# A Hyena-style mixer plus token MLP on one core: 16-bit sine phases, the state kernel loaded first, tap diagonals on GpSimd, and a new written-out order

## The chip, the cores and the metric

The kernel runs on one core of a Trainium2 chip. The core has a matrix engine (PE in the profile, with its weight loads as PEld), a vector engine (DVE), a scalar engine (ACT), a general engine (POOL, also called GpSimd) and SP, which here only issues DMAs. Each engine works through its own queue strictly in order, and the engines meet only through semaphores. The metric is the device time of one execution in microseconds; the kernel before has a median of 170.74 us over three runs (170.0 to 171.14).

## The reference

Two blocks, S = 2048 positions, D = 448 channels, F = 1792. All arrays are bf16.

```python
# block A, x = A_q:  q = layernorm(x)
k_shift = sum over t of k[s - t] * shift_k[:, 3 - t]      # 4 taps per channel
kv = k_shift * v
y  = causal convolution of kv with ssm_k, length 2048 (written as FFTs of length 4096)
y  = bf16(y) + kv * ssm_D
h  = x + q * y
# block B: z = layernorm(layernorm(h))
u  = gelu_tanh(einsum("bsd,sf->bdf", z, w1) + b1)         # mixes positions, not channels
out = h + transpose(einsum("bdf,fs->bds", u, w2) + b2)
```

## The kernel before

Position s is split as s = 16 q + r: q (0 to 127) is the partition, r (0 to 15) a row of 448 channels. All on-chip storage is one big array (`arena`), all matrix results lie in eight banks of `ps`, used singly or in pairs.

The long convolution is a two-stage Fourier transform done with matrix multiplies. Its pieces, named by the tags that the code and the text use:

- **tables** builds the sine and cosine tables: `E` (stage one, 32 tables of 128x128, made by the Sin function on ACT from integer phases that DVE prepares), `FW`, `MA`, `MB`, `MN` (stage two and its inverse), and the identity `ID`. The small tables need `pcf`, a column of bit fields of the partition number, which DVE makes in five short steps (L822 to L831); POOL then forms their phases (L854, L858), ACT takes the sine (L862), and POOL multiplies by a mask (L871).
- **loads** and **xload** fetch `ssm_k` (the state kernel, `KN`, four pieces), `k`, `v` and `x` (four pieces of 448 KB each), the taps and the biases. SP issues them.
- **kT** transposes the state kernel on PE (L1037), evicted by DVE or ACT.
- **kv** transposes `k` on PE (L965) into `KX`, and applies the four taps as PE multiplies with 64x64 diagonal matrices `DG` (L991); DVE multiplies the result by `v` (L1006). `DG` is an identity times the taps (L950, one DVE instruction of 128x1024).
- **k1**, **u1**: stage one of the transform, of the state kernel and of `kv`, 16 groups each (L1058), evicted to a ring of four buffers, mostly by ACT (L1068; four groups of k1 by DVE, L1066, which adds D there). For every second group three DMAs (L1074; two issued by POOL, one by SP) shuffle the ring into `TK` or `TU`.
- **k2**, **u2**: stage two (L1093), 16 steps each; the two results of a pair of steps go to ACT and DVE for eviction (L739, L742, L741).
- **i1**: DVE multiplies the two transforms (L1160, 16 products of 1.02 us apart), PE does the first inverse stage (L1177), ACT and DVE evict, and DMAs (L1201, and L1188 for the last pair) shuffle into `TZ`.
- **i2**: the second inverse stage for each r (L1303, L1309), followed by the gate with q and the two layer norms (DVE, ACT and POOL), which give `Q[r]`. The statistics of x (**q**, `bn_stats`, L1237) and four normalised rows (**xn**) are independent of the convolution.
- **mlp**: the two matrix products, 112 + 112 matmuls for the first (L1435, L1445), gelu on ACT (L1425), 238 for the second (L1457), the final add on DVE (L1460).

A step such as `k1.5` is the group 5 of its tag, and `k1.5:8` is instruction 8 of the step (here the eviction). The order of every engine's queue is written out by hand in the table `ORDER`, and the banks that each step takes in `SLOTS`; the replay in `schedule` (L297) follows both and only derives the waits from them. So a change of `ORDER` is a change of the program order on every engine.

## Time and profile before

| | us |
|---|---|
| median of three runs | 170.74 |
| profiled execution, span from first to last instruction | 168.7 |
| difference between the two | 2.0 |
| first k1 eviction on ACT starts | 14.32 |
| first k2 matmul starts | 34.96 |
| first i1 product on DVE starts | 50.05 |
| last i1 eviction on ACT ends | 70.83 |
| first mlp matmul starts | 78.25 |
| last mlp matmul's result reaches DVE | 165.81 |

The span is what the profiler saw of one execution, and its own time is that span; the runs are timed from outside and lie 2.0 us above it. Times in the text are counted from the span's start. A duration in a row is that of the instruction alone; instructions of one engine overlap a little, so that a row "x3 2.52" means 0.84 us for each in a sequence, where a single one shows 0.92. The granted clock of TensorE is 1.00 in all parts of the span.

### The profile page before, as it was taken

To read this page: it belongs to the slowest core of one execution; us is meant where nothing else is said; L and a number is where in the kernel's file an instruction comes from. 1 tells how busy PE (TensorE), PEld (TensorE's weight loads), DVE (VectorE), ACT (ScalarE), POOL (GpSimd) and SP (SyncE) were. 2 spreads that over 40 slices of the span, in tenths; PEclk is the share of its full clock that TensorE was granted. 3 is DMA by queue.
4 is the path that set the end of the run, shared out by engine and by line. 5 is a ranking of instruction groups with operands and counts; after the bars stand their busy time and mean duration, and the time that the engine had idled before them with its cause. 6 is when DMAs were issued, how large, how long until landed. Compare 5 with 4: busy or idle time off the path is not lost.

```text
span 168.7 us, 3563 instructions
## 1 busy us (share of the span) xinstructions
...
## 2 busy tenths in 40 slices
...
GB/s 142 421 310 385 286 278 348 312 355 132 211 134 325 248 197 186 196 152 290 388 402 400 424 421 422 418 112 0 0 0 12 46 54 54 54 2 56 54 54 54
DMA packets 15564, 35.15 MB, mean 208 GB/s; under 512 B 3804, under 2 KB 9644, under 8 KB 15548
## 3 DMA queue, kind: packets, MB, share of 16 engines
...
q10 hardware_dynamic: 144, 0.08, 0.2%
q14 instruction: 5, 0.04, 0.1%
...
## 4 chain that ended last, share of the span: by engine, by line
PE 62%; ACT 15%; DVE 10%; DMA 6%; issue 3%; POOL 1%; DVEq 0%; ACTq 0%; POOLq 0%
PE ps L1457 25%; PE ps L1435 13%; PE ps L1445 13%; ACT arena L738 7%; DMA arena<-arena 6%; ACT arena L1068 4%; ACT arena L739 4%; DVE arena L1160 2%; PE ps L1309 2%; PE ps L1058 2%; PE ps L1037 2%; PE ps L1093 2%; DVE arena L741 2%; DVE arena L837 1%; PE ps L1177 1%
## 5 line engine op out<-in xcount | busy, mean ns | idle before, releaser
L1460 DVE SCALAR_TENSOR_TENSOR arena<-ps,arena 128x448 bf16<-128x448 f32 (+2 forms) x17 | 11.1, 656 | 55.8 <-PE ps L1457 55.8
L1457 PE MATMUL ps<-arena 128*128 128x448 bf16 (+2 forms) x238 | 42.7, 342 | 0.0
L1457 PEld LDWEIGHTS ps<-arena 128*128 128x128 bf16 x238 | 33.3, 145 | 9.5
L1435 PE MATMUL ps<-arena 128*128 128x448 bf16 x112 | 23.5, 353 | 0.0
L738 ACT CAST arena<-ps 128x896 bf16<-128x896 f32 (+1 forms) x29 | 23.1, 933 | 0.0
L1068 ACT CAST arena<-ps 128x896 bf16<-128x896 f32 x24 | 20.2, 920 | 4.8 <-PE ps L1058 3.3
L1445 PE MATMUL ps<-arena 128*128 128x448 bf16 x112 | 22.3, 352 | 0.0
L1074 POOL DMA_DIRECT2D arena<-arena x32 | 17.7, 558 | 8.6 <-ACT arena L1068 8.5
L1425 ACT ACTIVATE arena<-ps,arena 128x448 bf16<-128x448 f32 x14 | 8.2, 632 | 19.3 <-PE ps L1445 10.3
L1093 PE MATMUL ps<-arena 128*64 128x448 bf16 x128 | 15.3, 361 | 2.0 <-ACT arena L739 0.9
L1435 PEld LDWEIGHTS ps<-arena 128*128 128x128 bf16 x112 | 10.7, 98 | 10.8 <-DVE arena L1388 1.3
L1445 PEld LDWEIGHTS ps<-arena 128*128 128x128 bf16 x112 | 11.0, 98 | 10.2
L1160 DVE TENSOR_TENSOR arena<-arena 128x1792 bf16<-128x1792 bf16 x16 | 16.5, 1084 | 0.0
L1177 PE MATMUL ps<-arena 64*128 64x448 bf16 x128 | 14.1, 351 | 1.1 <-ACT arena L738 0.5
L1058 PE MATMUL ps<-arena 128*32 128x448 bf16 x256 | 14.6, 355 | 0.5 <-ACT arena L1068 0.2
L1201 POOL DMA_DIRECT2D arena<-arena x16 | 9.3, 586 | 13.8 <-ACT arena L738 12.9
L1093 PEld LDWEIGHTS ps<-arena 128*64 128x64 f16 x128 | 5.3, 108 | 11.2 <-ACT arena L739 3.4
L1177 PEld LDWEIGHTS ps<-arena 64*128 64x128 f16 x128 | 5.2, 94 | 9.8 <-DVE arena L1160 3.1
L1388 DVE TENSOR_SCALAR arena<-arena 128x448 bf16<-128x448 f32 x16 | 7.6, 509 | 4.8 <-POOL arena L1381 4.8
L1058 PEld LDWEIGHTS ps<-arena 128*32 128x32 f16 x256 | 5.1, 95 | 7.8 <-ACT arena L1068 2.6
L1237 DVE BATCH_NORM_STATS2 arena<-arena 128x6 f32<-128x448 bf16 x16 | 9.4, 612 | 0.0
L739 ACT ACTIVATE arena<-ps 128x896 bf16<-128x896 f32 x10 | 8.6, 926 | 0.8 <-PE ps L1093 0.8
...
## 6 DMA issues: line engine op xcount, KB each, us to landing
...
```

Of the source, the lines that this page charges most:

```text
L738: return e.copy(out=dst(), in_=src())
L739: return e.activation(out=dst(), in_=src(), func=ACT.Copy, scale=scale)
L1058: op("pe", lambda e, W, b=b, r=r, q=q, x=x, c0=c0: e.matmul(PS[32 * q:32 * q + 32, b.slots[x], 0:D], E[:, 2 * r + x, c0:c0 + 32], src[:, r ...
L1068: return e.copy(out=dst, in_=Ppair(b)) if W == "act" else e.tensor_copy(out=dst, in_=Ppair(b))
L1074: shuf[tag].append(op(q_, lambda e, W, g=g, i=i, a=a, nu=nu, jh=jh: e.dma_start(T[a + i:a + i + 4 * nu - 3:4].rearrange("p (j k) c d -> p ...
L1093: op("pe", lambda e, W, b=bs[h], h=h, j=j, c=c, par=par: e.matmul(PS[64 * par:64 * par + 64, b.slots[c], 0:D], FW[:, 64 * c:64 * c + 64], ...
L1160: op("dve", lambda e, W, m=m, i=i: e.tensor_tensor(out=MR(m.slots[0]).rearrange("p (x y) d -> p x y d", x=2), in0=TU[:, i].unsqueeze(2).br ...
L1177: k = op("pe", lambda e, W, b=bs[h], m=ms[h], par=par, t=t, tab=tab, xy=xy, P=P: e.matmul(Pb(b, par), tab[P, :], MR(m.slots[0])[P, xy, :], ...
L1435: op("pe", lambda e, W, r=r, fc=fc, b=bs[fc]: e.matmul(Pb(b), W1A[:, r, 128 * fc:128 * fc + 128], Q[:, r, :], start=(r == 0), stop=(r == R ...
L1445: op("pe", lambda e, W, r=r, fc=fc, b=b: e.matmul(Pb(b), W1B[:, r, 128 * (fc - n0):128 * (fc - n0) + 128], Q[:, r, :], start=(r == 0), sto ...
L1457: op("pe", lambda e, W, r=r, fc=fc, b=b, d0=d0, d1=d1: e.matmul(Pb(b)[:, d0:d1], W2[fc // 7][:, fc % 7, r:S:R], G[:, fc, d0:d1], start=(fc ...
L1460: op("dve", lambda e, W, r=r, b=b, A=A, d0=d0, d1=d1: e.scalar_tensor_tensor(out=XR(r)[:, d0:d1], in0=Pb(b)[:, d0:d1], scalar=bm[:, r:r + ...
```

## The change

Four edits and a new order.

1. **Phases of `E` in 16 bits.** Before, DVE computes the phase of every table as a 32-bit product of 1024 elements, adds a quarter period, and masks, each twice. Now it computes one row of 128 as a 16-bit product, doubles the number of rows four times by 16-bit additions (128, 256, 512 and 1024 elements), and masks and shifts in six 16-bit instructions of 1024 elements. ACT takes the sines in four instructions of 1024 elements in place of two of 2048.
2. **Taps.** They are loaded as four contiguous rows by DMAs that ACT issues, transposed on PE (four small matmuls, `kv.0`) and evicted to `wsc`; POOL's cast goes. The diagonals `DG` may be made by DVE or POOL, and `ORDER` gives them to POOL.
3. **Loads.** The pieces of the state kernel are loaded ahead of three of the four pieces of `k`, one piece of x ahead of all of `v` and a second ahead of three of its four pieces; the biases later.
4. **b2** is used as bf16 (a DVE cast of 16 elements goes).
5. **`ORDER` and `SLOTS` are new on all engines.** k1 comes ahead of nearly all of the tap matmuls and u1; the table `FW`, its relatives and `pcf` come later; bn_stats of the first two pieces of x come earlier, others later; the small shuffles of i1 go behind the last large ones; the matmuls of the MLP are interleaved over r and over blocks.

```diff
 ORDER = {
     "pe": (
-        "dummy.0:1-9 kv.4:0-11 kv.3:0-7 kv.6:0-11 kv.5:0-7 kT.1:0-7 kT.0:0-3 kT.1:9-11 kT.0:4-7 kT.3:0-7 "
+        "dummy.0:1-9 kv.2:0-7 kv.3:0-11 kv.0:0 kT.0:0-7 kT.1:0-7 kT.1:9 kT.4:0-7 kT.1:10-11 kT.5:0-7 kT.2:0-7 "
...
-            for h in range(2):
-                sch.t0 = T_TH if h else -40.0
-                o_ph = (o_pi, o_TK)[h]
-                ph = view(o_ph, [2, 8, 128], i32)
-                op("dve", lambda e, W, h=h, ph=ph: e.tensor_tensor(
-                    out=ph[:, 1], in0=frow.unsqueeze(1).broadcast_to([128, 8, 128]),
-                    in1=srow[:, 8 * h:8 * h + 8].unsqueeze(2).broadcast_to([128, 8, 128]), op=ALU.mult),
-                   r=[(o_fr, 512), (o_s, 64)], w=[(o_ph + 4096, 4096)], n=HALF, kind="1x")
-                op("dve", lambda e, W, ph=ph: e.tensor_scalar(
-                    out=ph[:, 0], in0=ph[:, 1], scalar1=2048, scalar2=None, op0=ALU.add),
-                   r=[(o_ph + 4096, 4096)], w=[(o_ph, 4096)], n=HALF)
-                op("dve", lambda e, W, ph=ph: e.tensor_scalar(
-                    out=ph, in0=ph, scalar1=8191, scalar2=None, op0=ALU.bitwise_and),
-                   r=[(o_ph, 8192)], w=[(o_ph, 8192)], n=2 * HALF)
-                op("act", lambda e, W, h=h, ph=ph: e.activation(
-                    out=E[:, 16 * h:16 * h + 16, :].rearrange("p a (b c f) -> p a b c f", b=4, c=2).rearrange("p a b c f -> p (a b) c f"),
-                    in_=ph.rearrange("p c r (g f) -> p c (r g) f", f=16).rearrange("p c g f -> p g c f"),
-                    func=ACT.Sin, bias=bias[:, 0:1], scale=-SC),
-                   r=[(o_ph, 8192), (o_b, 4)], w=[(o_E + 4096 * h, 4096)], n=2 * HALF)
+            sch.t0 = -40.0
+            op("dve", lambda e, W: e.tensor_tensor(out=bq, in0=frow, in1=qcol.broadcast_to([128, 128]), op=ALU.mult),
+               r=[(o_fr, 256), (o_s, 4)], w=[(o_bq, 256)], n=128, est=150.0)
+            op("dve", lambda e, W: e.tensor_scalar(out=ph[:, 0], in0=bq, scalar1=511, scalar2=4, op0=ALU.bitwise_and,
+                                                   op1=ALU.logical_shift_left),
+               r=[(o_bq, 256)], w=[(o_ph, 256)], n=128)
+            for dst, o_, m in ((f2, o_f2, 2), (f4, o_f4, 4)):
+                op("dve", lambda e, W, dst=dst, m=m: e.tensor_scalar(out=dst, in0=frow, scalar1=m, scalar2=None, op0=ALU.mult),
+                   r=[(o_fr, 256)], w=[(o_, 256)], n=128, est=95.0)
+            for m, (fm, o_) in ((1, (frow, o_fr)), (2, (f2, o_f2)), (4, (f4, o_f4)), (8, (f8, o_f8))):
+                op("dve", lambda e, W, m=m, fm=fm: e.tensor_tensor(
+                    out=ph[:, m:2 * m], in0=ph[:, 0:m], in1=fm.unsqueeze(1).broadcast_to([128, m, 128]), op=ALU.add),
+                   r=[(o_ph, 256 * m), (o_, 256)], w=[(o_ph + 256 * m, 256 * m)], n=128 * m)
+                if m < 4:
+                    continue
+                h = m // 4 - 1
+                sch.t0 += 0.1
+                op("dve", lambda e, W, h=h: e.tensor_scalar(
+                    out=a1[:, 8 * h:8 * h + 8], in0=ph[:, 8 * h:8 * h + 8], scalar1=8191, scalar2=None, op0=ALU.bitwise_and),
+                   r=[(o_ph + 2048 * h, 2048)], w=[(o_a1 + 2048 * h, 2048)], n=HALF // 2)
+                op("dve", lambda e, W, h=h: e.tensor_scalar(
+                    out=a0[:, 8 * h:8 * h + 8], in0=ph[:, 8 * h:8 * h + 8], scalar1=2048, scalar2=None, op0=ALU.add),
+                   r=[(o_ph + 2048 * h, 2048)], w=[(o_a0 + 2048 * h, 2048)], n=HALF // 2)
+                op("dve", lambda e, W, h=h: e.tensor_scalar(
+                    out=a0[:, 8 * h:8 * h + 8], in0=a0[:, 8 * h:8 * h + 8], scalar1=8191, scalar2=None, op0=ALU.bitwise_and),
+                   r=[(o_a0 + 2048 * h, 2048)], w=[(o_a0 + 2048 * h, 2048)], n=HALF // 2)
+                for c, (src, o_src_) in enumerate(((a0, o_a0), (a1, o_a1))):
+                    op("act", lambda e, W, h=h, c=c, src=src: e.activation(
+                        out=E[:, 16 * h:16 * h + 16, :].rearrange("p a (b c f) -> p (a b) c f", c=2, f=16)[:, :, c, :],
+                        in_=src[:, 8 * h:8 * h + 8].rearrange("p r (g f) -> p (r g) f", f=16),
+                        func=ACT.Sin, bias=bias[:, 0:1], scale=-SC),
+                       r=[(o_src_ + 2048 * h, 2048), (o_b, 4)], w=[(o_E + 4096 * h, 4096, "E%d" % h)], n=HALF)
+                sch.t0 += 0.1
...
-            for i, c in enumerate((0, 1, 2, 3)):
+            for i, c in enumerate((3, 0, 1, 2)):
...
-            op(Dq, lambda e, W: e.dma_start(wsn[:, 0:3], A_shift_k[0:384].rearrange("(c p) j -> p c j", p=128)),
-               w=[(o_wsn, 24, "ws")], dmab=3072)
+            op("act", lambda e, W: e.dma_start(wsn[0:3], A_shift_k[0:384].rearrange("(c p) j -> c (p j)", c=3)),
+               w=[(o_wsn, 1024, "ws")], dmab=3072)
             for h in range(2):
-                op(Dq, lambda e, W, h=h: e.dma_start(wsn[64 * h:64 * h + 64, 3], A_shift_k[384:448]),
-                   w=[(o_wsn + 24, 8, "ws")], dmab=512)
+                op("act", lambda e, W, h=h: e.dma_start(wsn[3:4, 256 * h:256 * h + 256],
+                                                       A_shift_k[384:448].rearrange("(a p) j -> a (p j)", a=1)),
+                   w=[(o_wsn, 1024, "ws")], dmab=512)
...
             sch.t0 = -39.0
-            op("pool", lambda e, W: e.tensor_copy(out=wsc, in_=wsn.rearrange("p c j -> p (c j)")),
-               r=[(o_wsn, 32)], w=[(o_wsc, 64)], n=16)
+            b = _Buf(psum)
+            for j in range(4):
+                op("pe", lambda e, W, b=b, j=j: e.transpose(out=Pbf(b, 0)[:, 4 * j:4 * j + 4], in_=wsn[0:4, j:512:4],
+                                                           identity=ID[0:4, 0:4]),
+                   r=[(o_wsn, 1024), (o_ID, 256)], bw=[b], kind="tr", mode=4)
+            evac(lambda: wsc.rearrange("p (c j) -> p j c", j=4), lambda b=b: Pbf(b, 0)[:, 0:16].rearrange("p (j c) -> p j c", c=4),
+                 [(o_wsc, 64)], b, 16)
+            sch.t0 += 0.1
...
-            op("dve", lambda e, W: e.tensor_tensor(
+            op(("dve", "pool"), lambda e, W: e.tensor_tensor(
                 out=DG.rearrange("p c j d -> p (c j) d"), in0=I2.unsqueeze(1).broadcast_to([128, 16, 64]),
                 in1=wsc.unsqueeze(2).broadcast_to([128, 16, 64]), op=ALU.mult),
-               r=[(o_I2, 128), (o_wsc, 64)], w=[(o_DG, 2048)], n=1024, est=1700.0)
+               r=[(o_I2, 128), (o_wsc, 64)], w=[(o_DG, 2048)], n=1024, est={"dve": 1700.0, "pool": 2400.0})
...
-            op("pool", lambda e, W: e.tensor_tensor(out=bm, in0=qs[:, :, 0], in1=b2c, op=ALU.add),
-               r=[(o_qst, 256), (o_b2c, 64)], w=[(o_bm, 64)], n=16)
+            op("pool", lambda e, W: e.tensor_tensor(out=bm, in0=qs[:, :, 0], in1=b2n, op=ALU.add),
+               r=[(o_qst, 256), (o_b2n, 32)], w=[(o_bm, 64)], n=16)
```

Because `kv` now begins with the taps as a step of their own, its step numbers go up by one: the transposes of `k` are kv.2 to kv.9 and the tap matmuls kv.10 to kv.17. Lines of the changed program lie some 27 to 51 above those of the kernel before (L1068 becomes L1119, L1074 becomes L1125, L1237 becomes L1288).

Three places of the new order, on the engines that the rest waits for. First ACT's queue from its start to the first casts of k1; before (L847 is the Sin of `E`, L738 are evictions of `KX`, of the first `E` transpose and of the bias, L862 is the sine of the small tables, L1068 the casts of k1 and u1):

```order
L785 ACT_TABLE_LOAD
L785 ACTIVATE arena<-arena 128x1
L738 COPY arena<-ps 128x2x4x128 x3
L847 ACTIVATE arena<-arena 128x2048 x2
L738 COPY arena<-ps 128x1024
L738 CAST arena<-ps 128x14
L862 ACTIVATE arena<-arena 128x384
L1068 CAST arena<-ps 128x896 x20
```

and now (L936 and L939 issue the taps' DMAs, L892 is the Sin of `E`, L765 are evictions of `KX`, of the transposed state kernel and of the taps, L817 a one-element Sin, L1119 the casts of k1 and u1):

```order
L939 DMA arena<-in_A_shift_k_dram 1x256 x2
L765 ACT_TABLE_LOAD
L765 COPY arena<-ps 128x2x4x128
L892 ACT_TABLE_LOAD
L892 ACTIVATE arena<-arena 128x64x16
L765 COPY arena<-ps 128x8x128
L892 ACTIVATE arena<-arena 128x64x16 x2
L765 COPY arena<-ps 128x8x128
L765 CAST arena<-ps 128x4x4
L1119 CAST arena<-ps 128x896
L892 ACTIVATE arena<-arena 128x64x16
L817 ACTIVATE arena<-arena 128x1
```

The one-element Sin, which came first before, now stands behind the real ones, and there are two table loads in this part where there was one; the sines alternate with evictions of the state kernel.

Second, POOL's queue through the small tables and the shuffles of k1; before (L854 and L858 the phases of the small tables, L871 and L874 their masks, L943 the taps, L1074 the shuffles of k1 and u1):

```order
L946 MEMSET arena 128x2x3 x2
L854 TENSOR_SCALAR arena<-arena 128x128 x3
L858 TENSOR_TENSOR arena<-arena 128x384
L871 TENSOR_TENSOR arena<-arena 128x128 x3
L874 TENSOR_SCALAR arena<-arena 128x128
L943 CAST arena<-arena 128x16
L1074 DMA arena<-arena 8x4x1792 x26
```

and now, from the middle of the shuffles of k1 (L1125; the one between the first and second L900 is k1.9:9, the first two of the six are k1.15:9 and k1.13:9; L900 and L904 are the phases, L917 the mask of `FW`, L1296 a step of q):

```order
L1125 DMA arena<-arena 8x4x1792 x4
L900 TENSOR_SCALAR arena<-arena 128x128
L1125 DMA arena<-arena 8x4x1792
L900 TENSOR_SCALAR arena<-arena 128x128 x2
L1296 TENSOR_SCALAR arena<-arena 128x2
L904 TENSOR_TENSOR arena<-arena 128x384
L1125 DMA arena<-arena 8x4x1792 x6
L917 TENSOR_TENSOR arena<-arena 128x128
L1125 DMA arena<-arena 8x4x1792 x4
```

What stood ahead of all shuffles now stands between them, and the last shuffles of k1 are queued behind it. L900 waits for `pcf`, whose last step on DVE (L863) now stands behind the tap products of kv.10, kv.13, kv.11 and kv.17.

Third, DVE's queue from the last product of i1 to the first combination of i2; before (L1160 the product, L1237 and L1239 statistics of x, L1272 a row of xn, L1339 the combination):

```order
L1160 TENSOR_TENSOR arena<-arena 128x1792
L1237 BN_STATS arena<-arena 128x6 x4
L1239 BN_AGGR arena<-arena 128x2 x3
L1237 BN_STATS arena<-arena 128x6
L1239 BN_AGGR arena<-arena 128x2 x2
L1237 BN_STATS arena<-arena 128x6 x2
L1272 TENSOR_SCALAR arena<-arena 128x448
L1339 SCALAR_TENSOR_TENSOR arena<-ps,arena 128x448 x2
```

and now, the last part of the same stretch, behind four more statistics that follow the last product (L1288 and L1290 the statistics, L1311 a step of xn, L1323 a row of xn, L1390 the combination):

```order
L1288 BN_STATS arena<-arena 128x6
L1311 SCALAR_TENSOR_TENSOR arena<-arena 128x2
L1290 BN_AGGR arena<-arena 128x2 x2
L1288 BN_STATS arena<-arena 128x6
L1290 BN_AGGR arena<-arena 128x2
L1288 BN_STATS arena<-arena 128x6
L1290 BN_AGGR arena<-arena 128x2
L1323 TENSOR_SCALAR arena<-arena 128x448
L1288 BN_STATS arena<-arena 128x6 x2
L1390 SCALAR_TENSOR_TENSOR arena<-ps,arena 128x448 x2
```

Nine bn_stats now stand between the last product and the first combination, where there were seven.

40 lines of the change are left out of this document (22 added, 18 removed), and 194 rows, old and new, of tables (ORDER, SLOTS).

## The prediction

> **What bounds the kernel now.** I read the sums over stretches first, then the chain that ended last, then the queues of ACT, DVE and POOL in order of time. These stretches are cut at the first k1 cast, the last i1 eviction, the first mlp matmul and the last one (columns: stretch, length, busy us and count of PE, PEld, DVE, ACT, POOL).
>
> ```profile
> 14.32:70.83 56.51, 52.67 (x761) 23.96 (x753) 54.17 (x78) 51.25 (x62) 32.14 (x63) 1.00 0.76 254
> 0.89:68.92 68.03, 63.84 (x880) 31.98 (x880) 65.14 (x101) 58.92 (x70) 37.94 (x100) 1.00 0.80 269
> 78.25:165.81 87.56, 87.54 (x473) 55.92 (x474) 26.84 (x64) 22.11 (x48) 14.26 (x38) 1.00 0.44 172
> ...
> 123.70 42.08 PE ps L1457 x231
> ...
> 13.71 1.70 PE L1058 MATMUL ps<-arena 128*32 128x448 bf16 x32
> ```
>
> From 78.25 to 165.81 PE is idle for 0.02 us: a different order of the same matmuls can gain nothing there, and 2.89 us of tail follow that nothing here touches. (42.08 us for 231 is 0.182 each, the last ones being narrower.) So the change pays by the time at which the mlp starts. Before that, ACT is idle for 56.51 - 51.25 = 5.26 us between its first k1 cast and its last i1 eviction, and DVE for 68.03 - 65.14 = 2.89 us up to its last product. PE's row is as full, but its pieces overlap (32 matmuls of L1058 take 1.70 us, 0.41 for eight in sequence); the chain and the waits speak of ACT.
>
> ```profile
> 0.72 1.28 ACT L785 ACT_TABLE_LOAD   x1 [0.72 <-PEq L1505]
> 2.30 0.20 ACT L785 ACTIVATE arena<-arena 128x1 bf16<-128x1 f32 x1 [0.29 <-POOL arena L784]
> 5.74 2.84 ACT L738 COPY arena<-ps 128x1024 bf16<-128x1024 bf16 x3 [3.23 <-PE ps L965]
> 8.47 3.91 ACT L847 ACTIVATE arena<-arena 128x2048 f16<-128x2048 int32 x2
> 13.33 0.62 ACT L862 ACTIVATE arena<-arena 128x384 f32<-128x384 int32 x1
> 14.32 2.52 ACT L1068 CAST arena<-ps 128x896 bf16<-128x896 f32 x3 [0.38 <-PE ps L1058]
> ...
> 23.05 0.91 ACT L1068 CAST arena<-ps 128x896 bf16<-128x896 f32 x1 [2.33 <-PE ps L1058]
> 27.66 5.76 ACT L1068 CAST arena<-ps 128x896 bf16<-128x896 f32 x7 [1.02 <-PE ps L991]
> 37.89 2.58 ACT L739 ACTIVATE arena<-ps 128x896 bf16<-128x896 f32 x3 [0.23 <-PE ps L1093]
> 47.98 22.96 ACT L738 CAST arena<-ps 128x896 bf16<-128x896 f32 x28
> 70.83 1.02 ACT L738 COPY arena<-ps 128x1024 f16<-128x1024 f16 x1
> ```
>
> The reader sees ACT's gaps early (2.33 and 1.02 are the largest) and none at all in the last 23 us. In sequence a cast costs 0.84 (k1, u1), 0.86 (k2) or 0.82 (u2, i1).
>
> **When ACT starts on k1.** ACT now does one KX eviction (2.84 / 3 = 0.95), a second table load (1.28), three sines of 1024, two kernel evictions (0.95 each) and the taps (0.1) ahead of the first cast. A sine of 1024 is not in the trace; the rows of 2048 (1.95 each in sequence) and 384 (0.62) put it at 1.06. From 5.74: 0.95 + 1.28 + 3 x 1.06 + 1.90 + 0.10 = 7.41, so **13.15** in place of 14.32. The DMAs that ACT issues lie in its idle time before 5.74. The matmuls of k1.4 need all of the state kernel; those bytes are now fifth in line with 2240 KB where they were sixth with 2688.
>
> ```profile
> 10.00:15.00 5.00, 5.00 (x77) 3.71 (x78) 4.31 (x10) 4.62 (x6) 1.53 (x4) 1.00 1.05 346
> ...
> 11.94 1.18 PE L1037 MATMUL ps<-arena 64*128 64x64 bf16 x16
> ```
>
> At 346 GB/s 448 KB less are 1.3 us, so its last piece is there at 10.6, transposed and evicted by 12.2: hidden by ACT's queue. If it were not hidden, k1 would slip by what is missing.
>
> **ACT's load from there.** Its queue up to the last i1 eviction holds the 51.25 of before with two k2 evictions fewer (-1.72), and three KX evictions, a sine, a tiny sine and L862 more (2.85 + 1.06 + 0.15 + 0.62): 54.2. So the last i1 eviction ends at 13.15 + 54.2 = 67.35 plus ACT's idle time, which is the open number. Its ends are 0 and the 5.26 of before. Following the new queues in order with these durations I find: 0.7 where kv.6's eviction stands ahead of k1.14 and its transposes wait for banks; 0.8 where u1.0 stands behind kv.17 and kv.16 on PE; 0.7 around kv.12 and k2.13; 0.6 at u2.5, behind DVE's evictions of k2; and 0.9 in waits under 0.25. That is 3.7, nearer the upper row, and I take it: **71.05**, against 70.83.
>
> **DVE's side.** Removed: L837, L841 and L844 and DG.
>
> ```profile
> 4.66 0.69 DVE L841 TENSOR_SCALAR arena<-arena 128x1024 int32<-128x1024 int32 x1
> 17.29 1.22 DVE L950 TENSOR_TENSOR arena<-arena 128x1024 bf16<-128x1024 bf16 x1
> ...
> L741 DVE COPY arena<-ps 128x1024 bf16<-128x1024 bf16 x11 | 7.2, 684 | 0.3 <-PE ps L1037 0.3
> L742 DVE TENSOR_SCALAR arena<-ps 128x896 bf16<-128x896 f32 x6 | 6.3, 1082 | 0.4 <-PE ps L1093 0.4
> ...
> L837 DVE TENSOR_TENSOR arena<-arena 128x1024 int32<-128x1024 int32 x2 | 2.4, 1223 | 0.0
> L844 DVE TENSOR_SCALAR arena<-arena 128x2048 int32<-128x2048 int32 x2 | 2.4, 1224 | 0.0
> L860 DVE TENSOR_SCALAR arena<-arena 128x384 int32<-128x384 int32 x1 | 0.4, 365 | 0.1
> ```
>
> That is 2.4 + 1.4 + 2.4, or 5.8 in sequence, and 1.2. A 16-bit instruction of 1024 is in no row; it should lie between the 32-bit row of as many elements (0.69) and one of as many bytes (512 words, between 0.365 and 0.69: 0.43). I take 0.43, 0.34 in sequence; six of them and the additions (0.13 to 0.6) come to 3.7, with the upper end 5.4. So the phases save 0.4 to 2.1 and are ready at 7.1 to 8.0, while ACT reaches the first sine at 5.74 + 0.95 + 1.28 = 7.97: whatever DVE saves there is hidden behind the table load. From the rows of 128x1024 (0.65 in sequence) and 128x896 (1.06), DVE's queue up to the last product then has, beside the 1.2 of DG and the 2.1 of the phases, a KX and two kernel evictions less (-2.0), two i1 evictions less (-2.1), two each of k2 and u2 more (+4.2), one of E (+0.7), and two statistics and three aggregates less (-1.3): -3.8, or some 61 in place of 65.14. It is not the bound.
>
> The Trainium skill, "VectorE: DVE Perf Modes", section on the perf-mode tier table, has 16-bit tensor_scalar at four results a cycle and 32-bit at two, and the trace shows the latter (1024 in 0.60 in sequence); no 16-bit row of that size is here.
>
> **DG on POOL.** Rows of 128 (0.455) and 384 elements (1.00) give 2.1 ns for each further element, so 1024 take 2.4; the bounds are DVE's 1.22 and 2.67 (1.00 x 1024 / 384). It can start at 13.2 with the taps, and its first reader, kv.10, stands behind seven evictions, at 18.6: hidden, with 2.8 to spare.
>
> ```profile
> 7.14 0.17 DVE L831 CAST arena<-arena 128x6 f32<-128x6 int32 x1
> 7.42 2.05 POOL L854 TENSOR_SCALAR arena<-arena 128x128 int32<-128x128 int32 x3 [2.67 <-DVE arena L831]
> 9.55 1.00 POOL L858 TENSOR_TENSOR arena<-arena 128x384 int32<-128x384 int32 x1
> 14.03 1.29 POOL L871 TENSOR_TENSOR arena<-arena 128x128 f16<-128x128 f32 x3 [3.47 <-ACT arena L862]
> ...
> L1074 POOL DMA_DIRECT2D arena<-arena x32: 547/547/811, 16.3 to 45.7; - x32
> ...
> DMA to landing us min/median/max: 2.4/3.9/6.0
> ```
>
> **The added wait.** `pcf`, finished at 7.3 before, now comes on DVE after four k1 additions (4.2), five statistics (2.7), three KX evictions (2.0) and the products of four tap groups (4.2), plus 0.6 of small steps, from 13.0: 26.7, and with waits 27.2. POOL's L854 waits for it, and behind that POOL queues k1.9:9, the rest of L854, a step of q, L858, k1.15:9 and k1.13:9: 0.68 + 0.55 + 1.37 + 0.23 + 1.0 + 0.55 = 4.4 until k1.13:9 is issued, and 3.9 until it lands, at 35.5. k2.12 needs it. Without it PE would come to k2.12 at 35.6, after 20 casts (16.8), the KX evictions, sines and L862 (4.7) and 1.8 of idle on ACT, less 0.85 of lead. So it just fits.
>
> **The transition.** Before, the last product ends 1.9 before the last i1 eviction, and then:
>
> ```profile
> 68.92 2.19 DVE L1237 BATCH_NORM_STATS2 arena<-arena 128x6 f32<-128x448 bf16 x4
> 73.08 0.50 DVE L1272 TENSOR_SCALAR arena<-arena 128x448 f32<-128x448 bf16 x1
> 73.95 1.28 DVE L1339 SCALAR_TENSOR_TENSOR arena<-ps,arena 128x448 f32<-128x448 f32 x2 [0.37 <-PE ps L1309]
> ...
> 78.25 1.12 PE L1435 MATMUL ps<-arena 128*128 128x448 bf16 x5
> 79.20 0.54 PE L1309 MATMUL ps<-arena 128*128 128x448 bf16 x2
> ...
> L1408 SPq DMA_DIRECT2D arena<-in_B_w_dram x4: 378/460/508, 50.4 to 76.2; - x4
> ...
> DMA to landing us min/median/max: 4.8/12.9/21.5
> ```
>
> DVE was busy for 4.66 and waited 0.37 for PE. Now nine statistics (4.77), seven aggregates (0.56) and two steps of xn (0.5) come to 5.8, so the first combination starts at 71.05 - 1.9 + 5.8 = 74.95, 1.0 later, and the mlp with it. One more pair of i2 matmuls (0.38) stands ahead of the mlp, which takes it out of the dense part. The first weights, loaded from 50.4 before, are now issued behind the last shuffles, 1.4 after the last eviction, and land at best 4.8 later: 77.3, against a first mlp matmul at about 79.2. Hidden, with 1.9 to spare; a landing of 8 would cost 1.3.
>
> **The sum.** 168.7 + 1.0 - 0.38 = 169.3 for the profiled span. The median of the runs lies 2.0 above the span before, so **171.4**. A difference of 1% (1.7 us) is what a measurement of this kernel can tell from none.
>
> **Rivals.** *A packed ACT queue*: the new order takes ACT and DVE evictions so well in turn that ACT idles for 0.5 in place of 3.7. For it: the load of both engines together falls by 2, and the largest gap of before (2.33, tap matmuls on PE ahead of casts) is what the order breaks up. Against: the gaps then come from bank order, and there are as many banks. Time: 171.4 - 3.2 = 168.2; from 1.3 of idle down it is faster by over 1%.
>
> *POOL's queue jams* (slower): pcf comes 2 later than 27.2, since four tap products on DVE each wait for PE. Everything from k2.12 on moves by as much, as ACT has nothing else to do: 173.4. It decides from pcf at 27.3 on, microsecond by microsecond. For it: DVE's chain is bound to PE, and one shuffle has taken 6.0. Against: ACT's idle would partly be the same time.
>
> *The second table load costs more than its row.* After the first the next activation comes 0.30 later and was waiting for POOL, so the trace bounds the price to between 1.28 and 1.58. If the pipeline had to empty and fill as well, as long as the load itself, 1.3 more: 172.7. The Trainium skill, "ScalarE: Activation LUTs", section "What ACT_TABLE_LOAD costs", gives 1.28 for the load and some 2.66 with a drain, by which the sum would be 172.8; the first load here shows no room for it.
>
> *The edit does not do what it says*: 16-bit instructions run as long as 32-bit ones. The phases are then ready at 8.0 and ACT waits 0.1: 171.5.
>
> **Chances.** Forecast 0.41, packed queue 0.21, jam 0.27, table load 0.04, no 16-bit gain 0.07. The idle of the forecast (2.5 to 4.8) makes its own range 170.2 to 172.5. From the cases: faster by over 1% (below 169.0) 0.19, of which 0.17 are the packed queue's and 0.02 the forecast's edge; slower (above 172.4) 0.35, of which 0.24 are the jam's, 0.03 the table load's and 0.08 the forecast's; neither 0.46. The range reaches to both large rivals: 168.5 to 173.8.
>
> **What would show it.** First k1 cast on ACT at 13.1; two table loads ahead of it; ACT busy 54 and idle 3.7 up to the last i1 eviction at 71; L900 on POOL starting at 27 and the first k2 matmul at 35.6, with no wait for a DMA; first combination at 75; PE without gaps from 79 on. The prediction is wrong if ACT's idle is below 1.3, if k2 starts after 37, or if the interleaved mlp shows gaps on PE.

## The result and the profile after

The changed kernel takes 176.08 us (median of four runs, 175.51 to 178.35) against 170.8 us for the kernel before on the same chip: ratio 1.0305, 95% interval 1.0262 to 1.0347. It is **slower by 5.3 us**, above the range of the prediction. The profiled execution has a span of 173.7 us against 168.7, so the 5.0 us are in the profile too.

Up to the last eviction of i1 the profile is the forecast one. First the sums over three stretches, cut at the first k1 cast, the last i1 eviction, the first and the last mlp matmul (columns as in the prediction: stretch, length, busy us and count of PE, PEld, DVE, ACT, POOL, then PE's granted clock, DMA share, GB/s):

```profile
13.01:70.87 57.86, 54.34 (x804) 26.86 (x797) 54.84 (x85) 54.15 (x67) 37.27 (x85) 1.00 0.75 230
70.87:83.21 12.34, 8.70 (x36) 3.55 (x33) 8.40 (x28) 7.60 (x13) 6.23 (x12) 0.72 0.81 240
83.21:170.80 87.59, 87.53 (x471) 54.93 (x470) 25.15 (x60) 22.93 (x49) 14.47 (x37) 1.00 0.42 164
```

The kernel before, cut at the same three places:

```profile
70.83:78.25 7.42, 6.51 (x44) 3.39 (x44) 7.05 (x24) 7.29 (x12) 4.90 (x9) 1.00 0.60 175
```

The last stretch is as long as before (87.59 and 87.56) and PE idles in it for 0.06 us: the interleaved mlp neither gains nor loses. The first ends at the same time as before (70.87 and 70.83). The whole difference is in the middle: 12.34 in place of 7.42, with PE busy for 2.2 us more although it does less work there, and a granted clock of 0.72.

ACT's and POOL's queues in the first stretch:

```profile
6.28 1.28 ACT L892 ACT_TABLE_LOAD   x1
7.57 1.15 ACT L892 ACTIVATE arena<-arena 128x1024 f16<-128x1024 int16 x1
...
13.01 0.91 ACT L1119 CAST arena<-ps 128x896 bf16<-128x896 f32 x1 [0.31 <-PE ps L1109]
...
28.82 5.02 ACT L1119 CAST arena<-ps 128x896 bf16<-128x896 f32 x6 [2.02 <-DMA arena<-arena]
...
49.71 21.15 ACT L765 CAST arena<-ps 128x896 bf16<-128x896 f32 x26 [0.23 <-PE ps L1144]
```

```profile
13.45 1.91 POOL L1001 TENSOR_TENSOR arena<-arena 128x1024 bf16<-128x1024 bf16 x1 [9.39 <-DVE arena L999]
27.06 0.45 POOL L900 TENSOR_SCALAR arena<-arena 128x128 int32<-128x128 int32 x1 [1.17 <-DVE arena L863]
```

PE's queue behind the last i1 matmuls (L1158 the `E` transposes, L1354 the matmuls of i2 that need no shuffle, L1360 those that do: first the pairs of rows 1 and 0, which need all shuffles but the last group's, then the other rows), and the granted clock there (PE's busy time first, the clock third from the end):

```profile
69.82 1.22 PE L1158 MATMUL ps<-arena 128*128 128x128 f16 x19
...
72.23 0.92 PE L1354 MATMUL ps<-arena 128*128 128x448 bf16 x4
75.12 0.94 PE L1360 MATMUL ps<-arena 128*128 128x448 bf16 x4 [1.98 <-issue]
77.73 2.79 PE L1360 MATMUL ps<-arena 128*128 128x448 bf16 x7 [1.67 <-DMA arena<-arena]
```

```profile
74.00:76.00 2.00, 0.88 (x4) 0.32 (x4) 0.61 (x2) 1.49 (x2) 2.00 (x3) 0.97 0.75 182
76.00:78.00 2.00, 0.34 (x2) 0.13 (x2) 2.00 (x5) 0.00 (x0) 0.07 (x1) 0.50 1.02 350
78.00:80.00 2.00, 2.00 (x7) 0.81 (x6) 1.00 (x6) 0.72 (x1) 1.09 (x2) 0.50 0.72 216
80.00:82.00 2.00, 2.00 (x7) 0.85 (x6) 0.45 (x3) 1.79 (x4) 0.00 (x0) 0.50 0.91 317
82.00:84.00 2.00, 2.00 (x10) 0.81 (x8) 2.00 (x9) 1.26 (x4) 1.35 (x3) 0.82 0.77 205
```

The same part of the kernel before (L1107 the transposes, L1303 and L1309 the two kinds of i2 matmuls):

```profile
73.37 0.92 PE L1309 MATMUL ps<-arena 128*128 128x448 bf16 x4 [0.25 <-issue]
74.13 0.61 PE L1107 MATMUL ps<-arena 128*128 128x128 f16 x8
75.23 2.82 PE L1309 MATMUL ps<-arena 128*128 128x448 bf16 x14 [0.49 <-DMA arena<-arena]
```

Two things are to be seen. PE now stands still twice, for 1.98 and 1.67 us, where it waited 0.25 and 0.49 before: the first pair starts 1.75 later, the third 2.5 later. And then the clock is halved for some 6.8 us (75.9 to 82.7): seven matmuls take 2.79 us, where 14 took 2.82, and from the third pair to the mlp (83.21 - 77.73) it takes 5.48 us for 16 matmuls, where it took 3.02 (78.25 - 75.23) for 14 and one filler. 2.5 late from the waits, 2.5 from there on: 5.0.

Who issues what PE waits for? POOL's queue around the last shuffles, after and before (L1252 and L1201 are shuffles of 196 KB or 28 KB, L1239 and L1188 those of the last group, i1.16, 98 KB each; the two at 67.92 and the first two of the three at 66.36 are i1.6's, the ones at 69.53 and 69.47 begin i1.4's):

```profile
67.92 1.17 POOL L1252 DMA_DIRECT2D arena<-arena  x2 [1.74 <-ACT arena L765]
69.53 0.59 POOL L1252 DMA_DIRECT2D arena<-arena  x1 [0.45 <-ACT arena L765]
70.35 1.17 POOL L1239 DMA_DIRECT2D arena<-arena  x2 [0.22 <-issue]
```

```profile
66.36 1.71 POOL L1201 DMA_DIRECT2D arena<-arena  x3 [0.58 <-ACT arena L738]
69.47 1.15 POOL L1201 DMA_DIRECT2D arena<-arena  x2 [1.40 <-ACT arena L738]
70.61 1.20 POOL L1188 DMA_DIRECT2D arena<-arena  x2
```

And SP's, after (L1177 the four ct0 pieces of 4 KB, L1459 the first mlp weights, 896 KB):

```profile
65.61 2.82 SPq L1177 DMA_DIRECT2D arena<-arena  x4
69.27 1.42 SPq L1252 DMA_DIRECT2D arena<-arena  x2
70.89 2.41 SPq L1239 DMA_DIRECT2D arena<-arena  x2
73.34 0.75 SPq L1459 DMA_DIRECT2D arena<-in_B_w_dram  x1
```

The last shuffles are issued when they were issued before (69.5 and 70.9), but those of i1.6 only 1.6 us ahead of i1.4's where it was 3.1, and the first weights behind them at 73.34. From issue to landing POOL's two of i1.16 take 5.1 to 5.6 us, where they took 3.6 to 4.1. The row of the first pair names no releaser, but the landings do: POOL's i1.4 shuffle, issued at 69.53, lands 5.5 us later, at 75.03, and the pair starts at 75.12 (before: 3.8 us, landing at 73.28, start at 73.37). The third pair starts at 77.73, behind SP's second shuffle of i1.16, issued at 71.76 and landed at 77.68 (before: 71.68 and 75.18, start at 75.23). So there are four suspects: shuffles bunched at the end, weights in their way, SP's small pieces and ct0 pieces, and the clock.

### The profile page after: what moved, and what is told of

Its sections match the earlier page's. It is cut to its first block, busy times and chain, and to the rows that moved or that the text cites. A ratio compares the mean times of both kernels' runs of the same rounds, so it can differ in the third digit from the quotient of the medians.

```text
span 173.7 us, 3581 instructions
## 1 busy us (share of the span) xinstructions
PE 162.3 (93%) x1420; PEld 93.3 (54%) x1420; DVE 98.6 (57%) x195; ACT 93.4 (54%) x136; POOL 61.4 (35%) x157
## 4 chain that ended last, share of the span: by engine, by line
PE 53%; ACT 19%; DMA 17%; issue 4%; POOL 3%; SPq 1%; DVE 1%; ACTq 0%; POOLq 0%
PE ps L1508 24%; DMA arena<-arena 13%; PE ps L1496 12%; ACT arena L765 11%; PE ps L1486 9%; ACT arena L1119 6%; DMA arena<-in_A_ssm_k_dram 4%; PE ps L1360 3%; PE ps L1088 1%; PE ps L1144 1%; POOL arena L1299 1%; POOL arena L1432 1%; POOL arena L1125 1%; ACT arena L892 1%; SPq L933 1%
## 5 line engine op out<-in xcount | busy, mean ns | idle before, releaser
L1508 PE MATMUL ps<-arena 128*128 128x448 bf16 (+2 forms) x238 | 44.7, 343 | 0.0
L1511 DVE SCALAR_TENSOR_TENSOR arena<-ps,arena 128x448 bf16<-128x448 f32 (+2 forms) x17 | 10.6, 653 | 57.2 <-PE ps L1508 57.0
L1496 PE MATMUL ps<-arena 128*128 128x448 bf16 x112 | 27.6, 352 | 0.0
L1486 PE MATMUL ps<-arena 128*128 128x448 bf16 x112 | 27.0, 353 | 0.1
L765 ACT CAST arena<-ps 128x896 bf16<-128x896 f32 (+2 forms) x30 | 23.2, 980 | 0.7 <-PE ps L1144 0.7
L1119 ACT CAST arena<-ps 128x896 bf16<-128x896 f32 x24 | 20.4, 914 | 2.5 <-DMA arena<-arena 2.0
L1125 POOL DMA_DIRECT2D arena<-arena x32 | 18.1, 567 | 4.3 <-ACT arena L1119 1.8
L1252 POOL DMA_DIRECT2D arena<-arena x16 | 9.5, 598 | 13.8 <-ACT arena L765 13.8
L1360 PE MATMUL ps<-arena 128*128 128x448 bf16 x32 | 9.9, 448 | 3.6 <-issue 2.0
L1370 ACT ACTIVATE arena<-ps,arena 128x448 f32<-128x448 f32 x11 | 7.7, 722 | 5.3 <-PE ps L1360 5.1
L1057 DVE TENSOR_TENSOR arena<-ps,arena 128x512 bf16<-128x512 f32 (+1 forms) x16 | 9.3, 616 | 1.7 <-PE ps L1042 1.6
L765 ACT COPY arena<-ps 128x1024 bf16<-128x1024 bf16 (+1 forms) x9 | 9.4, 1096 | 1.3 <-PE ps L1016 1.3
```

The lines of the kernel that those rows point to most:

```text
L765: return e.copy(out=dst(), in_=src())
L1119: return e.copy(out=dst, in_=Ppair(b)) if W == "act" else e.tensor_copy(out=dst, in_=Ppair(b))
L1125: shuf[tag].append(op(q_, lambda e, W, g=g, i=i, a=a, nu=nu, jh=jh: e.dma_start(T[a + i:a + i + 4 * nu - 3:4].rearrange("p (j k) c d -> p ...
L1360: k = op("pe", lambda e, W, b=b, r=r, h=h: e.matmul(Pb(b), ET[:, 2 * r + h, :], TZ[:, r, h, :], start=(h == 0 and r >= NZ), stop=(h == 1)) ...
L1486: op("pe", lambda e, W, r=r, fc=fc, b=bs[fc]: e.matmul(Pb(b), W1A[:, r, 128 * fc:128 * fc + 128], Q[:, r, :], start=(r == 0), stop=(r == R ...
L1496: op("pe", lambda e, W, r=r, fc=fc, b=b: e.matmul(Pb(b), W1B[:, r, 128 * (fc - n0):128 * (fc - n0) + 128], Q[:, r, :], start=(r == 0), sto ...
```

## The experiments

All times below are medians of four runs (ten for e8) beside runs of the kernel before on the same chip (170.55 to 171.14). The kernels ran on several chips, so the ratio compares two of them better than the time does. The table reads one profiled execution of each; where the code of the transition is nearly the same, these readings repeat within 0.5 us (first pair +2.66 to +3.13 in e12, e13 and e14, +3.66 to +3.85 in e4, e5, e9 and e10), so that a difference of 0.5 at one pair is at the edge of what one profile shows. "End of i1" is the end of the last eviction on ACT (start of its row plus duration; the 70.83 given earlier for the kernel before is where ACT's next instruction starts); the next columns are the waits from there to the first pair of L1360, to the third, and to the first mlp matmul. Kernels made from another one carry its edits too.

| kernel | edit | time | ratio to before, 95% | end of i1 | first pair | third pair | mlp |
|---|---|---|---|---|---|---|---|
| before | | 170.8 | | 70.94 | +2.43 | +4.29 | +7.31 |
| changed | | 176.08 | 1.026 to 1.035 | 70.86 | +4.26 | +6.87 | +12.35 |
| e1 | 18 filler matmuls | 175.01 | 1.018 to 1.030 | 70.24 | +4.19 | +7.85 | +11.37 |
| e2 | weights early | 174.71 | 1.012 to 1.028 | 71.44 | +4.21 | +6.12 | +10.84 |
| e3 | small pieces early | 177.74 | 1.035 to 1.049 | 73.48 | +8.19 | | +13.84 |
| e4 | i1.6:9 on DVE | 175.32 | 1.021 to 1.032 | 70.85 | +3.66 | +7.40 | +12.12 |
| e5 | e2 and e4 | 173.59 | 1.010 to 1.023 | 70.79 | +3.85 | +6.31 | +9.83 |
| e6 | SP as before | 173.44 | 1.007 to 1.022 | 71.11 | +4.64 | +6.26 | +10.88 |
| e7 | e4, e6, fillers | 174.35 | 1.013 to 1.025 | 70.66 | +4.34 | +6.61 | +10.12 |
| e8 | before, weights late | 171.57 | 1.001 to 1.005 | 70.77 | +2.45 | +4.81 | +7.71 |
| e9 | e4, SP as before, ct0 early | 174.7 | 1.015 to 1.025 | 71.87 | +3.66 | +5.64 | +9.21 |
| e10 | e7 without fillers | 173.2 | 1.009 to 1.021 | 71.75 | +3.68 | +5.96 | +10.82 |
| e11 | e9, 8 fillers | 174.45 | 1.015 to 1.024 | 72.24 | +4.82 | +6.43 | +9.94 |
| e12 | SP as before, i1.6 first | 173.3 | 1.014 to 1.020 | 71.77 | +2.72 | +5.16 | +8.68 |
| e13 | e12, last four swapped | 175.52 | 1.026 to 1.031 | 74.44 | +3.13 | +5.33 | +10.06 |
| e14 | e12, A_ssm_k first | 177.11 | 1.027 to 1.044 | 76.55 | +2.66 | +5.27 | +8.78 |

### e1: the clock alone

```diff
-... i2.1:0-3 i2.10:0-1 i2.2:0-1 i2.45:0-1 ...
+... i2.1:0-3 warm.2:0 (to warm.11:0) i2.10:0-1 i2.2:0-1 warm.12:0 (to warm.19:0) i2.45:0-1 ...
```

> The changed kernel with 18 more matmuls of no use (448 columns each) on PE: 10 ahead of the first combination pair's L1360, 8 ahead of the third. They stand where PE was idle (73.2 to 75.1 and 76.1 to 77.7) and move no other instruction. Theory 'clock': the halved clock between 76 and 82.6 costs about 2.4 us of the 5.0; without the idle gaps it stays at 1.0, the landings stay at about 75.1 and 77.7, the first mlp matmul comes near 80.8 instead of 83.2, time 173.5 to 174. Rival 'landing alone' (the clock is only a label, or the PE work behind 77.7 is held by the landings of the w1a transfer): no gain, 175.8 to 176.5.

PE's queue and the clock with the fillers (L1262):

```profile
72.44 2.06 PE L1262 MATMUL ps<-arena 128*128 128x448 f16 x10
74.43 0.92 PE L1360 MATMUL ps<-arena 128*128 128x448 bf16 x4
75.18 1.68 PE L1262 MATMUL ps<-arena 128*128 128x448 f16 x8
78.09 3.67 PE L1360 MATMUL ps<-arena 128*128 128x448 bf16 x16 [1.23 <-DMA arena<-arena]
81.61 0.74 PE L1486 MATMUL ps<-arena 128*128 128x448 bf16 x3
```

```profile
76.00:78.00 2.00, 0.86 (x5) 0.23 (x3) 1.75 (x7) 0.00 (x0) 0.16 (x1) 1.00 0.81 285
78.00:80.00 2.00, 1.85 (x9) 0.81 (x10) 0.69 (x2) 1.29 (x2) 0.93 (x2) 1.00 0.61 159
```

The clock stays at 1.00 (mean 1.0 in all four runs, where the changed kernel has 0.97 to 0.98 in all four), and the 16 matmuls of the third pair and behind take 3.5 us up to the mlp in place of 5.5: the halved clock costs **2.0 us**, where 2.4 was expected. The time falls by only about 1, since the third pair comes 1.0 later after the end of i1 than without fillers. That half was not expected. e11 against e9 (+6.43 and +5.64) shows the same sign, with less to it, but e7 against e10 does not: SP's last shuffle landed 4.7 us after its issue with fillers and 5.2 without. So it is not shown that fillers on PE hold a DMA, and why e1's landing was late stays open.

### e2, e8: the first weights, moved both ways

```diff
# e2, SP of the changed kernel
-... xload.2:0 ct0.1:0-1 i1.1:22 ... i1.16:20 i1.16:19 w1a.0:0 i1.14:20 ...
+... xload.2:0 w1a.0:0 ct0.1:0-1 i1.1:22 ... i1.16:20 i1.16:19 i1.14:20 ...
# e8, SP of the kernel before
-... xload.2:0 xload.3:0 w1a.0:0 ct0.1:2 ... i1.16:19 i1.16:20 w1a.1:0 ...
+... xload.2:0 xload.3:0 ct0.1:2 ... i1.16:19 i1.16:20 w1a.0:0 w1a.1:0 ...
```

> The changed kernel with one DMA issue moved: the first 896 KB of mlp weights (w1a.0) go back on SP from behind the last shuffles of the interactions to right behind the loads of x, as in the kernel before. Theory 'weights in the way' (the 896 KB compete with the last shuffles and their rest): the last landing that PE waits for comes from 77.7 to about 76, time 173 to 174.5. Rival 'bunched shuffles' (the last shuffles are late because they are issued close behind one another, whatever else SP does): the landings stay at 75.1 and 77.7, time 175.5 to 176.5.

> The kernel before with one DMA issue moved the other way: the first 896 KB of mlp weights from its place behind the loads of x to right behind the last shuffles (as the changed kernel has it). Theory 'weights in the way': the last shuffles, which landed in 3.6 to 4.1, land up to 1 us later, and the weights themselves, issued at 72.4 and 7 to 8 us under way, become the last that the first mlp matmul waits for: it comes near 79.5 to 80.5 in place of 78.25, time 172 to 173. Rival 'bunching alone': less than 0.5 of loss, 170.5 to 171.2.

The third pair, in e2 and in e8:

```profile
77.56 4.89 PE L1360 MATMUL ps<-arena 128*128 128x448 bf16 x16 [0.98 <-DMA arena<-arena]
```

```profile
75.58 2.81 PE L1309 MATMUL ps<-arena 128*128 128x448 bf16 x14 [1.00 <-DMA arena<-arena]
```

With the weights early the third pair comes 0.75 sooner after the end of i1 (6.12 against 6.87) and the first does not move: in this trace the weights, issued 1.6 us or more behind the last group's shuffles, hold those alone. In the kernel before the opposite move costs the third pair 0.5 (4.81 against 4.29) and the mlp 0.4; its ratio of 1.003 is clear of 1 but far below what I expected (172 to 173), since the weights land 6.2 us after their issue, at 78.39, just ahead of the first mlp matmul (78.48). So they are a part, 0.5 to 0.75 us (1.1 between e4 and e5), and not the cause of the rest.

e2's four runs also show the clock by themselves: three have a mean clock of 0.99 and take 174.55 to 175.1, the fourth has 0.999 and takes 172.9. The same program gains about 1.9 us when the clock holds.

### e3, e6: SP's small pieces

```diff
# e3
-... xload.2:0 ct0.1:0-1 i1.1:22 ct0.1:4 ct0.1:2-3 ct0.1:5 i1.4:18 i1.14:22 i1.16:20 i1.16:19 w1a.0:0 i1.14:20 ...
+... xload.2:0 i1.1:22 i1.1:20 (to i1.12:20) ct0.1:0-1 ct0.1:4 ct0.1:2-3 ct0.1:5 i1.6:22 i1.4:18 i1.16:20 i1.16:19 w1a.0:0 ...
# e6: as e3, but with "w1a.0:0 ct0.1:0-1" left right behind xload.2:0
```

> The changed kernel with SP's small shuffle pieces (28 KB each, i1.k:20 and i1.k:22) issued as they become ready, as in the kernel before, ahead of the ct0 pieces, and the first weights still right behind the last shuffles. Theory 'pieces at the end' (SP waits 9.3 us for the ct0 transposes, so nine pieces are issued behind the last shuffles and rows 14 and 15 and the weights come late): last landing near 76 and no later wait, time 172.5 to 174.5. Rival 'bunched shuffles': landings stay at 75.1 and 77.7, time 175.5 to 176.5.

> The changed kernel with the whole of SP's order at the end of the interactions as in the kernel before: first mlp weights early, the two fills L1168 left where they are, the small pieces issued as they become ready, the four ct0 pieces behind those of i1.12. Theory 'pieces at the end': SP's two L1239 take 1.4 in place of 2.3 to 2.4, i1.16 lands within 4 us of its issue as in the kernel before (3.6 to 4.1), the third combination starts near 75.5 to 76, and with gaps that short the clock stays at 1.0: time 171.5 to 173. Rival 'weights alone': as the run with the weights moved, 174.7 (172.9 where the clock holds).

e3 made a wait of its own. Its edit also moved the two fills `ct0.1:0-1` from 50 to 68 us; they read the buffer that the four ct0 pieces overwrite, so these, and with them the first matmuls of i2, waited for the fills to land:

```profile
68.46 1.44 SPq L1167 DMA_DIRECT2D arena<-arena  x2
73.98 2.70 SPq L1176 DMA_DIRECT2D arena<-arena  x4
76.73 1.43 SPq L1251 DMA_DIRECT2D arena<-arena  x2
```

(L1167 are the fills, L1176 the pieces, L1251 the next shuffles.) It says nothing on the question; e6 does. With the pieces out of the way as well as the weights, the third pair stands at +6.26, no better than with the weights alone (+6.12): the small pieces are not the cause. e6's runs divide by the clock as e2's did: 172.12 and 172.56 at 1.0, 174.31 and 174.5 at 0.99.

### e4, e5, e12: bunched evictions

```diff
# e4: i1.6:9 from ACT to DVE, behind the product i1.3; e5: e2 and e4
# e12, PE, ACT and DVE (and SP as in e6; other banks for i1.6, u2.14, u2.15 and ct0.0)
-... i1.12:10-17 u2.14:0-3 u2.15:0-3 ct0.0:0-7 i1.6:1-8 i1.6:10-17 i1.4:0-7 ...
+... i1.12:10-17 i1.6:1-8 i1.6:10-17 u2.14:0-3 u2.15:0-3 ct0.0:0-7 i1.4:0-7 ...
-... i1.12:18 u2.15:5 u2.15:4 i1.6:9 i1.6:18 i1.4:8 ...
+... i1.12:18 i1.6:18 u2.15:5 u2.15:4 i1.4:8 ...
-... i1.2:0 ct0.0:8 i1.3:0 ...
+... i1.2:0 i1.6:9 ct0.0:8 i1.3:0 ...
```

> The changed kernel with one eviction of the interactions (i1.6:9) moved from ACT to DVE, as it stood in the kernel before, behind the product i1.3. Theory 'bunched shuffles' (ACT evicts six blocks in a row at the end, so the shuffles of i1.6 are issued 1 to 1.5 us later than before and those of i1.4 and i1.16 stand behind them): i1.6's and i1.4's shuffles are issued about 0.8 earlier and i1.4 lands near 74.2 instead of 75.1; the last two products come 1.1 later on DVE, which takes part of it back at i1.16; time 174.5 to 175.5. Rival 'weights in the way' or 'pieces at the end': 176 or a little more.

> The changed kernel with two edits tried singly before: the first mlp weights issued early on SP, and the eviction i1.6:9 on DVE. The first alone moved the landing of i1.16's shuffles some 0.7 earlier against the end of the evictions, the second that of i1.4 some 0.9. Theory 'two causes' (bunched shuffles and weights in the way each hold a landing): both gains show in one trace, i1.4 lands about 5.2 us after its issue and i1.16 about 5, first combination near 74.4, the third near 76.5, time 172.5 to 174. Rival 'one cause' (either edit frees the same DMA time): no better than the first alone, 174.4 to 175.

> The changed kernel with SP's order at the end of the interactions as in the kernel before, and with the group i1.6 worked off ahead of the last two blocks of u2 on PE and ACT (i1.6 then u2.14 and u2.15), its second eviction on DVE ahead of the ct0 copy, as the kernel before has it. Theory 'bunched shuffles': i1.6's shuffles are issued near 66.4 in place of 67.9, so that they are through before those of i1.4 start; i1.4 lands within 4.2 us of its issue, first combination about 2.5 after the last eviction (3.6 to 3.8 in the runs so far, 2.5 in the kernel before), third about 4.4 after it; time 171 to 172.3 where the clock holds. Rival 'something else holds the landings': 3.6 and 5.6 after the last eviction again, 172.3 to 173.5.

e4 takes 0.6 from the first pair (+3.66) and makes the third later (+7.40, with the weights still behind it); with the weights early (e5) the third is at +6.31. So moving one eviction helps the first pair alone, and by an earlier issue: i1.4's shuffle leaves POOL 1.1 us sooner (68.39) and lands 5.7 after that, no faster than before the edit. e12 restores the order of the kernel before, in which i1.6 goes ahead of the last two blocks of u2:

```profile
65.92 1.17 POOL L1248 DMA_DIRECT2D arena<-arena  x2 [0.94 <-ACT arena L761]
70.36 0.59 POOL L1248 DMA_DIRECT2D arena<-arena  x1 [3.28 <-ACT arena L761]
71.17 1.17 POOL L1235 DMA_DIRECT2D arena<-arena  x2 [0.22 <-issue]
```

```profile
73.45 0.92 PE L1350 MATMUL ps<-arena 128*128 128x448 bf16 x4
74.49 0.93 PE L1356 MATMUL ps<-arena 128*128 128x448 bf16 x4
76.93 3.67 PE L1356 MATMUL ps<-arena 128*128 128x448 bf16 x16 [1.51 <-DMA arena<-arena]
80.45 0.74 PE L1482 MATMUL ps<-arena 128*128 128x448 bf16 x3
```

i1.6's shuffles (65.92) are now issued 4.4 us ahead of i1.4's (70.36), and the first pair starts 2.72 after the end of i1, with no wait that the row shows: as in the kernel before (2.43). e13 and e14, which carry the edit too, show 3.13 and 2.66. The third pair follows to +5.16 (5.33, 5.27). **Bunching is the cause of the first late pair**, 1.5 us of it, and of about 1 us at the third (5.16 against 6.26 in e6). All sixteen profiles divide this way: where i1.6's first shuffle leaves POOL 3.1 to 4.4 us ahead of i1.4's (the kernel before, e8, e12, e13, e14), i1.4's lands 3.1 to 3.8 us after its issue; where it is 1.2 to 1.6 ahead (the other eleven), 5.2 to 6.4. Which part of the way is too narrow for the bunch, POOL's queue or the transfers themselves, is not separated. The clock held in all four runs of e12. Its time, 173.3, is nevertheless above what was expected (171 to 172.3), as is the third pair (4.4). The end of i1 is 0.9 later than in the changed kernel; ACT waits 1.54 and 1.03 for PE near the end of i1. But from the first k1 cast to the end of i1 e9, e10 and e11, without this edit, take as long (58.4 to 59.6 us, 58.8 in e12, 57.9 in the changed kernel), so it is not shown that the edit alone costs the 0.9.

### e7, e10, e11: fillers on top

> The changed kernel with SP's order as in the run before this one, the eviction i1.6:9 on DVE, and the 18 matmuls of no use in PE's gaps. Theory: landings near 74 and 75.5 and the clock at 1.0 throughout; the mlp starts near 79; time 171 to 172, the same as the kernel before, so that the whole 5.0 us is accounted for in the transition. Rival 'the rest lies elsewhere' (the interleaved mlp or the front): 173 or more although the mlp starts before 80.

> The run with SP's order, the eviction on DVE and the 18 matmuls of no use, without those 18. There the last shuffle's bytes had moved by 76, but the eight matmuls of no use held PE until 77.3. Theory: the third combination starts at 76 to 76.4, the mlp near 79.7, time 171.5 to 172.5 where the clock holds, and 2 more where it is halved after the gaps (1.2 and 1.0 long). Rival 'PE did not wait for the 18 matmuls': same as with them, 174 to 174.5.

> The first of these three with eight matmuls of no use (five ahead of the first combination, three ahead of the third), which fill 1.0 and 0.6 us of PE's gaps. Theory 'clock': no halved clock in any run, so the same fast runs as without them and none that is 2 slower; median 171 to 171.8. Rival: they hold PE longer than the landings do and cost 0.3 to 0.6.

e7 missed: the clock held, but the mlp came 2.8 later than in the kernel before. Its eight fillers ahead of the third pair ran until 77.27, although SP's last shuffle had landed at 76.15: they held PE themselves. e10, without them, has the third pair at +5.96 and then, in its profiled run, the halved clock; its runs at 1.0 take 172.33, 172.93 and 173.47, the one at 0.99 takes 174.78. e11's fillers kept the clock and gained nothing. Filling the gaps is no cure; what PE waits for has to come sooner.

### e9: the ct0 pieces

```diff
# PE, DVE; SP: ct0.1 and w1a.0 all ahead of the first i1 piece; ct0.0 takes bank 2 between k2.7 and u2.1
-... u2.0:0-3 u2.1:0-3 ...
+... u2.0:0-3 ct0.0:0-7 u2.1:0-3 ...
-... u2.5:5 u2.1:5 i1.0:0 ...
+... u2.5:5 ct0.0:8 u2.1:5 i1.0:0 ...
```

> The changed kernel with all that the kernel before has at the end of the interactions: SP's order with the first weights early and the small pieces as they become ready, i1.6:9 evicted on DVE, and in addition the transposes ct0.0 and their copy moved from 64 to 48 us (between two blocks of u2), so that the four ct0 pieces (L1177) leave SP's queue ahead of all shuffles of i1 in place of standing directly ahead of i1.4's and i1.16's. Theory 'ct0 pieces in the way': SP's two L1239 take 1.4 again, i1.4 and i1.16 land within 4.2 us of their issue (near 73.4 and 75.5, plus what the transposes cost in u2, up to 0.7), time 171 to 172. Rival 'something else holds the landings': i1.4 lands 5.5 to 6 and i1.16 4.5 to 5 after issue as in the run with every edit but this one, time 172 to 173.5.

The theory fell. The first pair is at +3.66, as in e10, which differs from it only in ct0, and the third at +5.64 against +5.96; SP takes 2.46 us to issue its two shuffles of i1.16. The ct0 pieces hold nothing. From the first k1 cast to the end of i1 it takes 0.45 longer than e10, which need not be the move: e7 and e10, alike up to there, differ by 0.6.

### e13, e14: the order of the last four, and the front

```diff
# e13, on top of e12
-SP:   ... i1.4:18 i1.16:20 i1.16:19 ...       POOL: ... i1.4:20 i1.16:22 i1.16:21 ...
+SP:   ... i1.4:18 i1.16:19 i1.16:20 ...       POOL: ... i1.4:20 i1.16:21 i1.16:22 ...
# e14, on top of e12
-SP:   loads.5:0 loads.1:0 loads.3:0 loads.2:0 loads.0:0 ...
+SP:   loads.1:0 loads.3:0 loads.5:0 loads.2:0 loads.0:0 ...
```

> The run before this one with the last four shuffles of 98 KB (i1.16) issued in the order of the kernel before on both queues: those that go to the partitions below 64 first, then the others (the changed kernel has it the other way round). Theory 'same half at once' (transfers to one half of the partitions share DMA engines, and with i1.4:20 in flight the upper half is loaded already): the third combination 0.4 to 1.0 earlier. Rival: no difference, within 0.5.

> The run with i1.6 first, with two of the four loads of the SSM kernels (A_ssm_k, two blocks of 128 rows or less) issued ahead of the first load of A_k on SP. Theory 'exposed front': in the changed kernel PE asks for A_ssm_k after 20 transposes of A_k in place of 40, near 6.0 in place of 7.3 us, and in some runs waits 0.4 to 2.0 us for it, which the whole program carries along; the earlier issue (0.45) shortens these waits, time 172.3 to 173 and less spread. Rival 'the waits lie elsewhere' (A_k now comes later, or the later wait of ACT for k1's shuffles, 0.7 to 2.5 us, takes it back): 173 to 174.

The order of the last four does not matter (+5.33 against +5.16). e13 is nevertheless 2.2 us slower than e12, and its profiled execution, 4.0 us longer than e12's, shows two reasons. The clock is halved from 80.3 to 83.7, and the mlp starts 10.06 behind the end of i1 in place of 8.68; two of the four runs have a mean clock of 0.99, where e12 has 1.0 in all. And the front is late: ACT's first k1 cast starts at 14.81 in place of 13.00, because PE waits twice for the state kernel (rows of PE; L1084 are its transposes):

```profile
8.52 0.72 PE L1084 MATMUL ps<-arena 128*128 128x128 bf16 x8 [0.70 <-DMA arena<-in_A_ssm_k_dram]
...
10.95 1.21 PE L1084 MATMUL ps<-arena 128*128 128x128 bf16 x16 [0.83 <-DMA arena<-in_A_ssm_k_dram]
```

In e14, with two pieces of the state kernel ahead of A_k, these waits are gone, and PE stands still for A_k instead:

```profile
6.72 2.03 PE L1012 MATMUL ps<-arena 128*128 128x128 bf16 x20 [1.80 <-DMA arena<-in_A_k_dram]
```

The first cast starts at 17.05, 4.05 later than in e12, i1 ends 4.8 later, the mlp starts 4.9 later, and the median is 3.8 longer (3.2 beside the kernel before on each chip): a cure it is not, but this trace shows that the front passes a late load on in full. Over the profiled executions of the changed kernel and the thirteen kernels made from it the first cast starts between 12.65 and 17.05. The profiled execution of the changed kernel itself was an early one (13.01).

None of these kernels is faster than the kernel before.

## Why the prediction was wrong

**The front was right in nearly every term.** First k1 cast 13.15 forecast, 13.01 measured; table load 1.28 and the sine directly behind it (7.57), so the rival of a dearer second load falls, and with it the 2.66 us that the Trainium skill, "ScalarE: Activation LUTs", section "What ACT_TABLE_LOAD costs", gives for a switch; a sine of 1024 1.05 to 1.15 (1.06); a 16-bit instruction of 1024 on DVE 0.42 to 0.53 (0.43), so the rival without a 16-bit gain falls; ACT's load 54.15 us (54.2) and its idle time 57.86 - 54.15 = 3.71 (3.7), so the packed queue falls too; last i1 eviction 70.87 (71.05); L863 at 26.78 and L900 at 27.06 (27.2), first k2 matmul at 35.69 (35.6), so POOL's queue did not jam; `DG` on POOL 1.91 (2.4) and hidden (by the prediction's own figures with 3.0 to spare, not 2.8). That the idle time sums to 3.7 is partly luck: its largest piece, 2.02 ahead of u1.0's cast at 28.82, is a wait for a shuffle of k1 to leave the ring buffer, where the prediction had 0.8 for PE, and the other pieces were smaller than forecast.

**The interleaved mlp was right as to gaps**: there are none. The 0.38 that the sum takes off is not there: 87.59 us, where 87.56 - 0.38 = 87.18 was forecast.

**The step that failed is "The transition".** It said that the first combination comes 1.0 later because nine bn_stats stand ahead of it on DVE, and that the first weights are "hidden, with 1.9 to spare". The first mlp matmul was to start at about 79.2 and started at 83.21. Each sentence asked about the wrong thing.

- DVE was not late. Its row at the first combination, L1390, reads:

```profile
75.70 1.27 DVE L1390 SCALAR_TENSOR_TENSOR arena<-ps,arena 128x448 f32<-128x448 f32 x2 [1.39 <-PE ps L1360]
```

  It was ready at 74.3 and waited 1.39 for PE. The forecast time, 74.95, missed by 0.75 only, but by luck. What PE waited for was the landing of i1.4's shuffles, which the sum had no term for: I took them to land as before, since they are issued as before. The runs show that it also counts how close behind others they are issued: with i1.6 1.6 us ahead i1.4 lands 5.5 us after its issue and the first pair comes 4.26 after the last eviction, with i1.6 4.4 ahead 3.2 and 2.72. The order that did this (u2.14 and u2.15 ahead of i1.6) is a line in the table of the change, on an engine that waits, and I had not read it.
- The weights were hidden, but by luck: issued at 73.34, they landed 7.2 us later, at 80.6, where 77.3 was forecast at best. Had the mlp started at 79.2 they would have held it by 1.4, much as the prediction says of a landing of 8. And their bytes delay the last shuffles by 0.5 to 0.75 us (e8, e2); the step asked only whether they come in time, not whom they slow down.
- No step had a term for the clock. It was 1.00 in all of the trace before; two waits of under 2 us each halved it for 6.8 us, which costs 2.0 (e1). With the 0.5 that the matmuls from the third pair to the mlp take longer in any case, it doubles a loss of 2.5 to 5.0. Without it the time would have stood at the edge of the range (176.08 - 2.0 = 174.1 against 173.8).

**Where the 5.3 us are.** Clock 2.0 (e1, and the runs of e2 and e6 that kept it). Bunching about 1.5 at the first pair and 1.0 at the third, which is the one that counts; weights 0.5 to 0.75 at the third. These three make up 3.5 to 3.75 of the 5.0 of the profile; undoing bunching and weights (e12) brought the distance to the kernel before on the same chip from 5.3 to 2.75, with the clock holding by itself.

**What stays open.** e12's span is 2.2 above that of the kernel before: 0.8 at the end of i1, which the edit may have brought in, and 1.4 behind it. Of this the third pair is 0.9 (+5.16 against +4.29): the last group's shuffles still land later than in the kernel before, and neither the weights, the small pieces, the ct0 pieces nor their order explains it. The other 0.5 lies between the third pair and the mlp, where 16 matmuls stand in place of 14 and one filler. And the medians of the changed kernels lie 0.5 to 1.8 above their best runs; the clock is a part of this (e2, e6), and a late front is a shown cause in two traces (e13, e14), not in every run.
